# Attention stages on half-array tiles: two heads side by side in place of block-diagonal q and padded v

## Chip, cores, metric

One core of one Trainium2 chip. The metric is the device time of one execution in microseconds (us). A ratio is the mean time of one kernel's fast runs over the mean of the other's in the same rounds, so it is not quite the ratio of the medians that stand beside it.

## The reference

Block-wise linear attention with decay, over 4 batches, 8 heads, 768 positions and head size 64, and then a feed-forward layer with `h * cos(h)` between 512, 2048 and 512 columns. Cut to what matters:

```python
for b in range(nb):                       # blocks of 64 along the sequence
    intra = einsum('bhic,bhjc->bhij', qb, kb) * Dmask
    intra = einsum('bhij,bhjd->bhid', intra, vb)
    inter = einsum('bhid,bhde->bhie', qb * lam_pow, kv_state)
    out[:, :, sl] = intra + inter
    kv_state = lam_block * kv_state + einsum('bhsd,bhse->bhde', kb * rev_pow, vb)
x = out.transpose(0, 2, 1, 3).reshape(3072, 512)
h = x @ w_in                              # 512 -> 2048
return (h * cos(h)) @ w_out               # 2048 -> 512
```

## The kernel before

The kernel takes the sequence in 24 blocks of 128 positions (6 a batch). A planner in Python orders all instructions of all engines before they are emitted; attention of later blocks is mixed with the feed-forward matmuls of earlier ones. A head is 64 wide and the array is 128 by 128, so heads go in pairs p, and the array is filled with zeros where the two heads of a pair must not mix: q is copied into a block-diagonal tile `q_bd`, v is scaled into a padded tile `v_pad`, the state `kv_bd` is block-diagonal too. Cuts are marked `...`.

```python
def prep_v():                                             # GpSimd, two instructions
    for i in range(2):
        nc.gpsimd.tensor_mul(v_pad[n % NV][:, i::2, i * D:(i + 1) * D], src[:, i::2, :],
                             v_scale[:, c, i::2]...to_broadcast([P, NP, D]))
...
def transposes_out(sides):                                # VectorE, PSUM to SBUF
    nc.vector.tensor_copy(live["qkT", n][:, sides], live["t", n][:, sides])

def transposes_bd():                                      # VectorE, SBUF to SBUF, two instructions
    for i in range(2):
        h = slice(i * D, (i + 1) * D)
        nc.vector.tensor_copy(q_bd[n % NQ][h, :, i, :], t[h, 0, :, :])

def scores(half):                                         # 2 matmuls of 256 columns
    t = bank("ps_s", [P, 4, P], F32)                      # one bank, two buffers
    for i in range(2):
        p = 2 * half + i
        nc.tensor.matmul(t[:, 2 * i:2 * i + 2, :], lhsT=live["qkT", n][:, 1, p, :],
                         rhs=q_bd[n % NQ][:, p, :, :], start=True, stop=True)
...
def update():                                             # 4 matmuls of 128 columns
    for p in range(NP):
        nc.tensor.matmul(kv_ps[:, p, :], lhsT=live["k_b", n][:, 2 * p:2 * p + 2, :], rhs=both, ...)

def values(half):                                         # 2 x (1 inter + 2 intra) matmuls of 128
    for p in (2 * half, 2 * half + 1):
        if c:
            nc.tensor.matmul(t[:, p, :], lhsT=kv_bd[(n - 1) % NK][:, p, :],
                             rhs=live["qkT", n][:, 0, p, :], start=True, stop=False)
        for i in range(2):
            nc.tensor.matmul(t[:, p, :], lhsT=v_pad[n % NV][:, 2 * p + i, :],
                             rhs=live["s_m", n][:, 2 * p + i, :], ...)
```

## Time and profile before

| | before |
|---|---|
| time, median | 235.72 us of 3 runs at first, 235.46 us of 4 with the changed kernel's |
| span of the profiled run | 233.6 us, granted clock 0.999 |
| TensorE busy | 220.6 us, 94% |
| VectorE, ScalarE, GpSimd busy | 63%, 46%, 31% |

TensorE's records overlap, so its busy share hides small gaps. The useful measure is the slot: the difference of the starts of two matmuls that follow each other. Two rows of the costliest groups (line, engine, operation, output and input, shapes, count, then busy us and mean ns):

```profile
L250 POOL TENSOR_TENSOR v_pad<-v_f,v_scale 128x256 bf16<-128x256 f32 x48 | 29.1, 626 | 46.7 <-PE ps_o L341 30.1
L303 DVE TENSOR_TENSOR s_m<-ps_s,mask 128x512 bf16<-128x512 f32 x48 | 31.3, 684 | 4.2 <-PE ps_s L296 4.1
```

GpSimd (POOL) makes v in two instructions of 0.63 us a block. VectorE (DVE) masks the scores, and the idle time before that is put down to the score matmuls.

### The profile page before, as it was taken

The page shows a single profiled execution, that of the slowest core. Times are in us where ns is not written, and L with a number is a line of the kernel's source. Part 1 is how long each engine was busy: PE and PEld are TensorE (multiplying, and loading weights), DVE is VectorE, ACT ScalarE, POOL GpSimd, SP SyncE. Part 2 cuts the span into 40 slices and gives each one's busy share as a digit, 9 for nine tenths or more (in the row PEclk, how much of TensorE's full clock was granted, in tenths as well). Part 3 has the DMA queues.
Part 4 walks back from the last instruction along what each step waited for, and adds up shares of the span by engine and source line. Part 5 has one row for each costly group of instructions (what it writes and reads, how often), then busy time and mean ns, then how long its engine had stood idle before and what let it go on. Part 6 is the DMA issues. An engine that isn't in the chain of part 4 may idle for free.

```text
span 233.6 us, 4414 instructions
## 1 busy us (share of the span) xinstructions
PE 220.6 (94%) x1698; PEld 131.2 (56%) x1698; DVE 148.3 (63%) x279; ACT 106.6 (46%) x179; POOL 71.7 (31%) x108
## 2 busy tenths in 40 slices
PE   4887998899999999999999999999999999999993
PEld 4777543457776655555555555555555454556541
DVE  5577487087999998986685585685674563423210
ACT  5453676123445464554444445345345435544420
POOL 2569200486758665333314314412000000000000
PEclk9999999999999999999999999999999999999999
DMA  6997999999999999999562110110011011111112
GB/s 123 222 198 120 208 191 203 225 219 217 254 222 248 222 219 225 243 218 201 137 158 68 48 45 1 48 46 8 37 48 45 0 48 45 45 45 48 45 45 90
DMA packets 82868, 29.64 MB, mean 127 GB/s; under 512 B 75552, under 2 KB 79904, under 8 KB 82848
## 3 DMA queue, kind: packets, MB, share of 16 engines
q1 hardware_dynamic: 78480, 25.05, 48.6%
q0 software_dynamic: 4224, 4.19, 11.0%
q8 instruction: 13, 0.21, 0.4%
q10 hardware_dynamic: 144, 0.13, 0.2%
q14 instruction: 7, 0.06, 0.1%
HBM read 27.27 MB, written 6.29 MB: 144 GB/s over the span
## 4 chain that ended last, share of the span: by engine, by line
PE 71%; DVE 11%; DMA 10%; POOL 3%; ACT 2%; issue 1%; POOLq 0%
PE ps_f L410 30%; PE ps_h L372 26%; DMA w_out_sb<-in_moe_w_out_dram 8%; PE ps_s L296 4%; PE ps_t L266 4%; PE ps_o L341 4%; DVE q_bd L277 3%; DVE g L385 3%; DVE s_m L303 2%; DVE qkT L271 2%; PE ps_o L338 1%; PE ps_kv L316 1%; DMA lam_bc<-in_lam_dram 1%; POOL w_in_sb L214 1%; DVE kv_bd L325 1%; POOL w_out_sb L217 1%
## 5 line engine op out<-in xcount | busy, mean ns | idle before, releaser
L379 ACT ACTIVATE cos<-ps_h,halfpi 128x512 f32<-128x512 f32 (+1 forms) x107 | 66.3, 624 | 73.5 <-PE ps_h L372 73.4
L385 DVE TENSOR_TENSOR g<-ps_h,cos 128x512 bf16<-128x512 f32 (+1 forms) x107 | 64.5, 609 | 49.2 <-ACT cos L379 48.0
L410 PE MATMUL ps_f<-w_out_sb,g 128*128 128x512 bf16 x368 | 92.8, 379 | 1.4 <-ACT o_sb L423 0.7
L372 PE MATMUL ps_h<-xT,w_in_sb 128*128 128x512 bf16 (+1 forms) x428 | 93.7, 347 | 0.1
L372 PEld LDWEIGHTS <-w_in_sb 128*128 128x128 bf16 x448 | 43.0, 98 | 36.0 <-issue 0.4
L410 PEld LDWEIGHTS <-g 128*128 128x128 bf16 x384 | 35.9, 98 | 34.4 <-issue 2.2
L250 POOL TENSOR_TENSOR v_pad<-v_f,v_scale 128x256 bf16<-128x256 f32 x48 | 29.1, 626 | 46.7 <-PE ps_o L341 30.1
L303 DVE TENSOR_TENSOR s_m<-ps_s,mask 128x512 bf16<-128x512 f32 x48 | 31.3, 684 | 4.2 <-PE ps_s L296 4.1
L235 POOL TENSOR_TENSOR q_s<-q_f,q_scale 128x512 bf16<-128x512 f32 x23 | 24.0, 1043 | 22.5 <-PE ps_f L410 18.7
L271 DVE COPY qkT<-ps_t 128x1024 bf16<-128x1024 bf16 (+1 forms) x28 | 17.2, 614 | 17.3 <-PE ps_t L266 16.9
L423 ACT COPY o_sb<-ps_f 128x512 f32<-128x512 f32 x23 | 13.5, 586 | 21.7 <-PE ps_f L410 21.7
L277 DVE COPY q_bd<-qkT 64x512 bf16<-64x512 bf16 x48 | 19.6, 409 | 0.7
L341 PE MATMUL ps_o<-s_m,v_pad 128*128 128x128 bf16 x192 | 19.7, 221 | 0.4 <-DVE s_m L303 0.4
L350 ACT CAST xT<-ps_o 128x512 bf16<-128x512 f32 x24 | 14.0, 585 | 13.1 <-PE ps_o L341 13.0
L296 PE MATMUL ps_s<-q_bd,qkT 128*128 128x256 bf16 x96 | 15.6, 279 | 2.7 <-DVE qkT L271 1.8
L244 POOL CAST k_b<-k_f 128x512 bf16<-128x512 f32 x20 | 12.4, 620 | 17.6 <-issue 13.3
L341 PEld LDWEIGHTS <-v_pad 128*128 128x128 bf16 x192 | 14.9, 99 | 3.5 <-issue 0.5
L338 PE MATMUL ps_o<-qkT,kv_bd 128*128 128x128 bf16 x80 | 15.3, 219 | 0.0
L296 PEld LDWEIGHTS <-qkT 128*128 128x128 bf16 x96 | 8.8, 99 | 9.7 <-DVE q_bd L277 2.2
L325 DVE CAST kv_bd<-ps_kv 64x256 bf16<-64x256 f32 x32 | 13.4, 418 | 1.2 <-PE ps_kv L316 1.0
L468 PE MATMUL ps_h<-ident 128*128 128x64 bf16 x226 | 12.1, 211 | 1.6 <-POOL ident masks.py:199 1.6
L468 PEld LDWEIGHTS <-ident 128*128 128x128 bf16 x226 | 10.8, 111 | 1.8 <-POOL ident masks.py:199 1.6
(39 smaller groups left out, 93.1 us busy)
## 6 DMA issues: line engine op xcount, KB each, us to landing
q_f<-in_q_dram SPq DMA_DIRECT2D x24, 256.0 KB, 4.8
k_f<-in_k_dram SPq DMA_DIRECT2D x24, 256.0 KB, 4.8
v_f<-in_v_dram SPq DMA_DIRECT2D x24, 256.0 KB, 4.9
out_dram<-o_sb SPq DMA_DIRECT2D x23, 256.0 KB, 2.0
w_in_sb<-in_moe_w_in_dram POOLq DMA_DIRECT2D x4, 512.0 KB, 8.4
w_out_sb<-in_moe_w_out_dram POOLq DMA_DIRECT2D x4, 512.0 KB, 15.5
out_dram<-o_sb SPq DMA_DIRECT2D x1, 128.0 KB, 1.7
out_dram<-o_sb ACTq DMA_DIRECT2D x1, 128.0 KB, 1.7
```

The lines of the kernel that those rows point to most:

```text
L235: eng.tensor_mul(t, live.pop(("q_f", n)), q_scale[:, c, :].unsqueeze(2).to_broadcast([P, H, D]))
L250: nc.gpsimd.tensor_mul(v_pad[n % NV][:, i::2, i * D:(i + 1) * D], src[:, i::2, :], v_scale[:, c, i::2].unsqueeze(2).to_broadcast([P, NP, D]))
L271: nc.vector.tensor_copy(live["qkT", n][:, sides], live["t", n][:, sides])
L277: nc.vector.tensor_copy(q_bd[n % NQ][h, :, i, :], t[h, 0, :, :])
L296: nc.tensor.matmul(t[:, 2 * i:2 * i + 2, :], lhsT=live["qkT", n][:, 1, p, :], rhs=q_bd[n % NQ][:, p, :, :], start=True, stop=True)
L303: nc.vector.tensor_mul(live["s_m", n][:, 4 * half:4 * half + 4, :], live.pop(("s", n, half)), mask.unsqueeze(1).to_broadcast([P, 4, P]))
L341: nc.tensor.matmul(t[:, p, :], lhsT=v_pad[n % NV][:, 2 * p + i, :], rhs=live["s_m", n][:, 2 * p + i, :], start=(i == 0 and c == 0), stop=( ...
L372: ins = nc.tensor.matmul(t[:, :cols], lhsT=w_in_sb[:, kd, f * P:(f + 1) * P], rhs=live["xT", i][:, kd, :cols], start=(kd == 0), stop=(kd = ...
L379: nc.scalar.activation(c[:, :cols], live["h", i, f][:, :cols], AF.Sin, bias=halfpi)
L385: nc.vector.tensor_mul(live["g", i][:, f, :cols], live.pop(("h", i, f))[:, :cols], live.pop(("c", i, f))[:, :cols])
L410: nc.tensor.matmul(live["f", i, j], lhsT=live["g", i][:, f, j * P:(j + 1) * P], rhs=w_out_sb[:, f, :], start=(f == 0), stop=(f == KF - 1))
L468: nc.tensor.matmul(idle_ps[:, :cols], lhsT=ident, rhs=ident[:, :cols], start=True, stop=True)
```

## The change

The intent is to let two heads use the array at the same time. Scores contract over 64 rows, so head 0 takes the upper half of the array's rows and head 1 the lower half. State and values have 64 output columns, so the two heads take the two halves of the columns. Then q needs no block-diagonal copy and v no padding. The diff, cut to its core:

```diff
-    BUFS = {... "ps_s": 2, ...}
+    BUFS = {... "ps_s": 1, ...}          # one buffer, now of two banks
-    v_pad = [...]; q_bd = [...]
...
         def prep_v():
-            for i in range(2):
-                nc.gpsimd.tensor_mul(v_pad[n % NV][:, i::2, i * D:(i + 1) * D], src[:, i::2, :], ...)
+            nc.gpsimd.tensor_mul(live["v_s", n], live.pop(("v_f", n)), ...)
...
-        def transposes_bd():
-            for i in range(2):
-                nc.vector.tensor_copy(q_bd[n % NQ][h, :, i, :], t[h, 0, :, :])
...
+        def scores():
+            t = bank("ps_s", [P, 2, NP, P], F32)
+            for p in range(NP):
+                for i, h in enumerate(halves):
+                    nc.tensor.matmul(t[:, i, p, :], lhsT=live["qkT", n][h, 1, p, :], rhs=live["qkT", n][h, 0, p, :], ...)
...
             def update():
                 for p in range(NP):
+                    for i, h in enumerate(halves):
+                        nc.tensor.matmul(kv_ps[h, p, :], lhsT=live["k_b", n][:, 2 * p + i, :],
+                                         rhs=live["v_s", n][:, 2 * p + i, :], ...)
...
+        def values():                     # all inter matmuls first, full array; then the tiles
+            for p in range(NP if c else 0):
+                nc.tensor.matmul(t[:, p, :], lhsT=kv_bd[(n - 1) % NK][:, p, :], rhs=live["qkT", n][:, 0, p, :], ...)
+            for p in range(NP):
+                for i, h in enumerate(halves):
+                    nc.tensor.matmul(t[h, p, :], lhsT=live["v_s", n][:, 2 * p + i, :], rhs=live["s_m", n][:, i, p, :], ...)
```

The planner's durations change as well: a stage on tiles is booked with 0.15 us on top, and the pacing constant of a block goes from 1.78 to 1.35 us.

More of the change, by code (lines that the diff above doesn't have):

```diff
@@ L14 @@
 ALU = mybir.AluOpType
+ATT = 1.35
 TILES = [4, 2, 4, 4, 4, 4, 2]
@@ L114 @@
     first = [sum(TILES[:i]) for i in range(len(TILES) + 1)]
-    BUFS = {"ld": 4, "tok": 3, "ps_t": 1, "ps_s": 2, "ps_o": 1, "ps_h": 2, "ps_f": 1, "cos": 2, "o_sb": 3}
+    BUFS = {"ld": 4, "tok": 3, "ps_t": 1, "ps_s": 1, "ps_o": 1, "ps_h": 2, "ps_f": 1, "cos": 2, "o_sb": 3}
     ctx.enter_context(tc.manual_schedule())
@@ L140 @@
     nc.vector.memset(halfpi, math.pi / 2.0)
-    NV, NQ, NK = 3, 2, 2
-    v_pad = [consts.tile([P, H, P], BF16, name=f"v_pad{i}") for i in range(NV)]
-    q_bd = [consts.tile([P, NP, 2, P], BF16, name=f"q_bd{i}") for i in range(NQ)]
+    NK = 2
     kv_bd = [consts.tile([P, NP, P], BF16, name=f"kv_bd{i}") for i in range(NK)]
-    for t in v_pad + q_bd + kv_bd:
+    for t in kv_bd:
         nc.vector.memset(t, 0.0)
@@ L163 @@
     WCH = 4
-    kv_ps = psum.tile([P, NP, P], F32, tag="ps_kv", name="ps_kv")
-    pl = Planner({"ps_t": 1, "ps_s": 2, "ps_o": 1, "ps_h": 2, "ps_f": 1, "cos": 2, "o_sb": 3,
-                  "q_f": 4, "k_f": 4, "v_f": 4, "q_s": 3, "k_b": 3, "qkT": 3, "s_m": 3})
+    kv_ps = psum.tile([P, NP, D], F32, tag="ps_kv", name="ps_kv")
+    pl = Planner({**BUFS, "q_f": 4, "k_f": 4, "v_f": 4, "q_s": 3, "k_b": 3, "v_s": 3, "qkT": 3, "s_m": 3})
     MM = lambda cols, n=1: n * (cols / 2400.0 + 0.0025)
+    SW = 0.15
+    halves = [slice(i * D, (i + 1) * D) for i in range(2)]
     live = {}
-    unit = [MM(n * P, 4 * KF) + MM(DM, KF * n) + 1.78 * n for n in TILES]
+    unit = [MM(n * P, 4 * KF) + MM(DM, KF * n) + ATT * n for n in TILES]
     begins = [sum(unit[:i]) for i in range(len(unit) + 1)]
@@ L223, in add_w @@
         _, w_t[which, c] = dma("POOL", 2.6, 0.9, emit, prio, deps)
-    prep, T, To, Tb, Sc, So, V, Vo, U, Uo = ({} for _ in range(10))
+    prep, T, To, Sc, So, V, Vo, U, Uo = ({} for _ in range(9))
     def add_attention(n):
@@ L247, in prep_v @@
         def prep_v():
-            src = live.pop(("v_f", n))
-            for i in range(2):
-                nc.gpsimd.tensor_mul(v_pad[n % NV][:, i::2, i * D:(i + 1) * D], src[:, i::2, :],
-                                     v_scale[:, c, i::2].unsqueeze(2).to_broadcast([P, NP, D]))
+            live["v_s", n] = toks.tile([P, H, D], BF16, tag="v_s", name="v_s")
+            nc.gpsimd.tensor_mul(live["v_s", n], live.pop(("v_f", n)),
+                                 v_scale[:, c, :].unsqueeze(2).to_broadcast([P, H, D]))
         a = pl.add("DVE" if n == 0 else "POOL", 0.69 if n == 0 else 1.05, [load_t["q_f", n]], prep_q, pa(-0.9), get="q_s")
@@ L256, in add_attention @@
         issue_t["k_f", n].frees = [b]
-        d = pl.add("POOL", 1.2, [load_t["v_f", n], V.get(n - NV), U.get(n - NV)], prep_v, pa(-0.9))
+        d = pl.add("POOL", 1.05, [load_t["v_f", n]], prep_v, pa(-0.9), get="v_s")
         issue_t["v_f", n].frees = [d]
@@ L271, in transposes_out @@
             nc.vector.tensor_copy(live["qkT", n][:, sides], live["t", n][:, sides])
-        def transposes_bd():
-            t = live["qkT", n]
-            for i in range(2):
-                h = slice(i * D, (i + 1) * D)
-                nc.vector.tensor_copy(q_bd[n % NQ][h, :, i, :], t[h, 0, :, :])
         Tq = pl.add("PE", MM(P, 4), [a], lambda: transposes(0), pa(-0.05), get="ps_t")
@@ L288, in add_attention, with scores_out @@
         Tq.frees = [To[n]]
-        Tb[n] = pl.add("DVE", 0.6, [first_out, Sc.get((n - NQ, 1))], transposes_bd, pa(-0.01 if early else 0.1))
-        for half in range(2):
-            def scores(half=half):
-                t = bank("ps_s", [P, 4, P], F32)
-                for i in range(2):
-                    p = 2 * half + i
-                    nc.tensor.matmul(t[:, 2 * i:2 * i + 2, :], lhsT=live["qkT", n][:, 1, p, :],
-                                     rhs=q_bd[n % NQ][:, p, :, :], start=True, stop=True)
-                live["s", n, half] = t
-            def scores_out(half=half):
-                if half == 0:
-                    live["s_m", n] = toks.tile([P, H, P], BF16, tag="s_m", name="s_m")
-                nc.vector.tensor_mul(live["s_m", n][:, 4 * half:4 * half + 4, :], live.pop(("s", n, half)),
-                                     mask.unsqueeze(1).to_broadcast([P, 4, P]))
-            Sc[n, half] = pl.add("PE", MM(2 * P, 2), [Tb[n], To[n]], scores, pa(0.2 + 0.1 * half), get="ps_s")
-            So[n, half] = pl.add("DVE", 0.69, [Sc[n, half]] + ([So[n, 0]] if half else []), scores_out,
-                                 pa(0.25 + 0.1 * half), get=None if half else "s_m")
-            Sc[n, half].frees = [So[n, half]]
+        def scores():
+            t = bank("ps_s", [P, 2, NP, P], F32)
+            for p in range(NP):
+                for i, h in enumerate(halves):
+                    nc.tensor.matmul(t[:, i, p, :], lhsT=live["qkT", n][h, 1, p, :], rhs=live["qkT", n][h, 0, p, :],
+                                     start=True, stop=True)
+            live["s", n] = t
+        def scores_out(i):
+            if i == 0:
+                live["s_m", n] = toks.tile([P, 2, NP, P], BF16, tag="s_m", name="s_m")
+            nc.vector.tensor_mul(live["s_m", n][:, i], live["s", n][:, i], mask.unsqueeze(1).to_broadcast([P, NP, P]))
+        Sc[n] = pl.add("PE", MM(P, 4) + SW, [first_out, To[n]], scores, pa(0.2), get="ps_s")
+        for i in range(2):
+            So[n, i] = pl.add("DVE", 0.69, [Sc[n]] + ([So[n, 0]] if i else []), partial(scores_out, i),
+                              pa(0.25 + 0.1 * i), get=None if i else "s_m")
+        Sc[n].frees = [So[n, 0], So[n, 1]]
         if c < NB - 1:
@@ L313, in update @@
                 for p in range(NP):
-                    vp = v_pad[n % NV][:, 2 * p, :]
-                    both = bass.AP(tensor=vp.tensor, offset=vp.offset, ap=[list(vp.ap[0]), [P + D, 2], [1, D]])
-                    nc.tensor.matmul(kv_ps[:, p, :], lhsT=live["k_b", n][:, 2 * p:2 * p + 2, :], rhs=both,
-                                     start=(c == 0 and p == 0), stop=True, skip_group_check=True)
+                    for i, h in enumerate(halves):
+                        nc.tensor.matmul(kv_ps[h, p, :], lhsT=live["k_b", n][:, 2 * p + i, :],
+                                         rhs=live["v_s", n][:, 2 * p + i, :],
+                                         start=(c == 0 and p == 0), stop=True, skip_group_check=True)
@@ L319, in update_out @@
             def update_out():
-                for i in range(2):
-                    h = slice(i * D, (i + 1) * D)
-                    if early:
-                        nc.scalar.copy(kv_bd[n % NK][h, :, h], kv_ps[h, :, h])
-                    else:
-                        nc.vector.tensor_copy(kv_bd[n % NK][h, :, h], kv_ps[h, :, h])
+                for h in halves:
+                    (nc.scalar.copy if early else nc.vector.tensor_copy)(kv_bd[n % NK][h, :, h], kv_ps[h])
             last = next((Uo[m] for m in (n - 1, n - 2) if m in Uo), None)
-            U[n] = pl.add("PE", MM(P, 4), [b, d, last], update, pa(0.3))
+            U[n] = pl.add("PE", MM(D, 4) + SW, [b, d, last], update, pa(0.3))
@@ L329, in add_attention @@
             Uo[n] = pl.add("ACT" if early else "DVE", 0.85, [U[n], V.get(n - NK + 1)], update_out, pa(0.4))
         b.frees = [T[n]] + ([U[n]] if c < NB - 1 else [])
-        def values(half):
-            if half == 0:
-                live["o", n] = bank("ps_o", [P, NP, P], F32)
-            t = live["o", n]
-            for p in (2 * half, 2 * half + 1):
-                if c:
-                    nc.tensor.matmul(t[:, p, :], lhsT=kv_bd[(n - 1) % NK][:, p, :],
-                                     rhs=live["qkT", n][:, 0, p, :], start=True, stop=False)
-                for i in range(2):
-                    nc.tensor.matmul(t[:, p, :], lhsT=v_pad[n % NV][:, 2 * p + i, :],
-                                     rhs=live["s_m", n][:, 2 * p + i, :],
-                                     start=(i == 0 and c == 0), stop=(i == 1))
+        def values():
+            t = live["o", n] = bank("ps_o", [P, NP, P], F32)
+            for p in range(NP if c else 0):
+                nc.tensor.matmul(t[:, p, :], lhsT=kv_bd[(n - 1) % NK][:, p, :], rhs=live["qkT", n][:, 0, p, :],
+                                 start=(p == 0), stop=False, skip_group_check=True)
+            for p in range(NP):
+                for i, h in enumerate(halves):
+                    nc.tensor.matmul(t[h, p, :], lhsT=live["v_s", n][:, 2 * p + i, :], rhs=live["s_m", n][:, i, p, :],
+                                     start=(p == 0 and c == 0), stop=True, skip_group_check=True)
@@ L350, in values_out @@
             nc.scalar.copy(live["xT", i][:, :, j * P:(j + 1) * P], live.pop(("o", n)))
-        v0 = pl.add("PE", MM(P, 6 if c else 4), [So[n, 0], d, Uo.get(n - 1) if c else None],
-                    lambda: values(0), pa(0.5), get="ps_o")
-        V[n] = pl.add("PE", MM(P, 6 if c else 4), [So[n, 1], v0], lambda: values(1), pa(0.6))
+        V[n] = pl.add("PE", MM(P, 8 if c else 4) + SW, [So[n, 0], So[n, 1], d, Uo.get(n - 1) if c else None],
+                      values, pa(0.5), get="ps_o")
         So[n, 0].frees = [V[n]]
-        first_out.frees = [V[n]]
+        first_out.frees = [V[n], Sc[n]]
+        d.frees = [V[n]] + ([U[n]] if c < NB - 1 else [])
         Vo[n] = pl.add("ACT", 0.6, [V[n]] + ([h_last[i - 2]] if i >= 2 else []), values_out, pa(0.7))
-        v0.frees = [Vo[n]]
+        V[n].frees = [Vo[n]]
     h_last, o_last, hid_t = {}, {}, {}
@@ L407, in project @@
                     if f0 == 0:
-                        live["f", i, j] = bank(tag, [P, DM], F32)
+                        live["f", i, j] = bank("ps_s", [P, 2, DM], F32)[:, 0, :] if tag == "ps_s" else bank(tag, [P, DM], F32)
                     for f in range(f0, f0 + U4):
```

## The prediction

> **What bounds the kernel now.** I read the page first, then the chain, the engine shares by window, the timelines of TensorE and VectorE, and the waits. The page gives the suspect: the matmul engine is busy for 94% of the span, at full clock throughout.
>
> ```profile
> PE 220.6 (94%) x1698; PEld 131.2 (56%) x1698; DVE 148.3 (63%) x279; ACT 106.6 (46%) x179; POOL 71.7 (31%) x108
> ...
> PE   4887998899999999999999999999999999999993
> ...
> DVE  5577487087999998986685585685674563423210
> ```
>
> A busy PE need not be full, because matmul records overlap, so I count slots from starts in the timeline. These are PE rows (start, duration, operation) of one attention block among feed-forward matmuls, from late in the run:
>
> ```profile
> 131.36 0.22 PE L338 MATMUL ps_o<-qkT,kv_bd 128*128 128x128 bf16 x1
> 131.42 0.27 PE L341 MATMUL ps_o<-s_m,v_pad 128*128 128x128 bf16 x2
> ...
> 132.03 1.03 PE L372 MATMUL ps_h<-xT,w_in_sb 128*128 128x512 bf16 x4
> 132.90 0.39 PE L266 MATMUL ps_t<-ident,q_s 128*128 128x128 bf16 x4
> 133.12 1.03 PE L410 MATMUL ps_f<-w_out_sb,g 128*128 128x512 bf16 x4
> ...
> 136.79 0.39 PE L316 MATMUL ps_kv<-v_pad,k_b 128*128 128x128 bf16 x4
> 137.02 1.03 PE L410 MATMUL ps_f<-w_out_sb,g 128*128 128x512 bf16 x4
> 137.88 0.60 PE L296 MATMUL ps_s<-q_bd,qkT 128*128 128x256 bf16 x4
> 138.32 1.03 PE L372 MATMUL ps_h<-xT,w_in_sb 128*128 128x512 bf16 x4
> ```
>
> Differences of starts: four matmuls of 512 columns take 0.865 us (216 ns each), four of 256 take 0.44 us, four of 128 take 0.22 to 0.23 us (56 ns each), and the twelve of the values stage take 132.03 - 131.36 = 0.67 us. An attention block therefore occupies PE for 0.446 (eight transposes) + 0.437 (scores) + 0.223 (state) + 0.67 (values) = 1.78 us.
>
> Is PE really full? From 45 us to the last matmul's end, about 227 us in the chain, there are 182 us. In them fall the 384 projections less the 20 issued before, 364 x 0.216 = 78.7; the hidden layer without the first tile's 64, 256 x 0.216 + 128 x 0.109 = 69.3; and 20 blocks (numbers 4 to 23) x 1.78, less 7 absent state or inter stages of 0.223, = 34.0. The sum is 182: PE has next to no hole from 45 us on. I find holes of some 2.6 us in its timeline, all between 47 and 89 us, so the count is right to about 1%.
>
> The first 45 us are another matter: attention of the first four blocks, then the first hidden tile, and then the wait for the second weight matrix.
>
> ```profile
> 24.04 18.26 DMA w_out_sb<-in_moe_w_out_dram
> 42.34 1.04 PE ps_f L410 x4
> ```
>
> In that stretch the DMA engines are 99% busy; no attention arithmetic makes this arrive sooner. From about 201 us no attention is left. So the change can act on PE between 45 and 201 us, on 20 of 24 blocks. VectorE is nearly full as well between 60 and 85 us:
>
> ```profile
> 60.00:65.00 5.00, 5.00 (x54) 4.00 (x53) 4.88 (x12) 2.43 (x6) 3.41 (x5) 1.00 1.19 252
> 65.00:70.00 5.00, 4.63 (x50) 3.73 (x49) 4.88 (x11) 2.23 (x6) 2.82 (x4) 1.00 0.98 222
> 70.00:75.00 5.00, 4.80 (x49) 3.57 (x48) 4.88 (x12) 2.33 (x7) 4.26 (x7) 1.00 1.08 241
> ```
>
> (The columns are the window, its length, then busy us of PE, weight load, DVE, ACT and POOL.) That is where the holes lie.
>
> **What the Trainium skill says.** (1) "TensorE: Matmul & The Clock Gate", section "Back-to-back issue gap": a warm matmul of N columns takes N/2.4 + 2.5 ns. The trace agrees: 216 ns at 512 and 56 ns at 128. (2) The same page, section "Part 3: Packing small matmuls", says that matmuls on different tiles start about 4 ns apart and run together; nothing in this trace uses tiles. (3) "TensorEngine Tiling (Array Packing)", section "Key Properties": "Changing tiling mode (not just tile) drains the TensorE". No duration is given, and the trace has no switch. (4) The same page, section "Restrictions": column tiling disables fast weight load. Every load in this trace is the full 128x128 form, so what a 64-column load costs is not to be seen here either. Points 3 and 4 are the uncertainty of this case.
>
> One number can be read from the trace, though: how fast small load-and-matmul pairs go at all. The 64-column keep-awake matmuls, each with its own weight load:
>
> ```profile
> 21.21 0.66 PE L468 MATMUL ps_h<-ident 128*128 128x64 bf16 x17
> ...
> 23.47 0.31 PE L468 MATMUL ps_h<-ident 128*128 128x64 bf16 x5
> ```
>
> Twelve more take 0.35 us: 29 ns for one load plus matmul, and I take that as the pace that tiled instructions cannot beat.
>
> **The change, part by part.** Scores: four matmuls of 256 columns against a half-zero q become eight of 128 on two half-row tiles. Perfect pairs would take 4 x 56 = 0.223 us; at 29 ns an instruction 8 x 29 = 0.233. Saved: 0.437 - 0.233 = 0.204 us. State update: four matmuls of 128 columns become eight of 64 on two half-column tiles. Perfect pairs would take 0.117 us, but eight at 29 ns take 0.233: saved -0.01. Values: eight of 128 with padded v become eight on half-column tiles, 0.233 for 0.446: saved 0.213. The four inter matmuls and the transposes stay. Over the 20 blocks (16 with an update): 20 x 0.204 - 16 x 0.01 + 20 x 0.213 = 8.2 us off PE before any drain. A block then costs about 1.37 us; the diff's new pacing constant of 1.35 (1.78 before) fits that.
>
> Against it stand the switches. Neighbours in the PE order are full-array matmuls, so each tiled stage has one switch in and one out: (20 + 16 + 20) x 2 = 112. Each costs d: 0 to perhaps 100 ns. The record of a lone matmul reaches about 160 ns beyond its slot (0.22 us against 0.056), which bounds what emptying the array should take without a reload of weights. The diff's planner books 0.15 us for each stage, thus 75 ns for a switch; it may be a cautious guess. I choose d = 35 ns as an estimate, 3.9 us in all. Net on PE: 8.2 - 3.9 = 4.3 us.
>
> VectorE loses the two copies into the block-diagonal q:
>
> ```profile
> L277 DVE COPY q_bd<-qkT 64x512 bf16<-64x512 bf16 x48 | 19.6, 409 | 0.7
> ```
>
> This is 19.6 us, or 0.8 us a block, and 0.8 to 1.4 us for a pair between 60 and 89 us, exactly where VectorE is full. The five start-up memsets (2.4 us) go as well, but the first q there waits for ACT. VectorE off the path is worth only the PE holes it causes: a third to a half of the 2.6 us, say 0.9. Against that, scores of a block now need both banks free and the values wait for both masked halves; with feed-forward work to fill in, I take zero. POOL forms v in one instruction of about 1.04 us (the q row's 1043 ns) instead of two of 0.61; POOL is 31% busy and worth nothing, except a few tenths before the issue of the second weight matrix, whose transfer is DMA-bound: zero. Evacuations and state copies keep their sizes.
>
> Sum: 4.3 + 0.9 = 5.2 us, so 235.7 - 5.2 = 230.5 us, about 2.2% less.
>
> **Rivals.** (a) Tiles overlap well and a switch is nearly free (d under 15 ns): 8.2 + 0.9 less up to 1.7, so 226.6 to 228.3 us. With perfect pairs even 225. For it: the tuned-looking 1.35. (b) The drains eat the gain: at d = 75 ns they are 8.4 us, and only the VectorE relief is left: about 235 us. For it: the planner's own 0.15 us. (c) Column-tile weight loads lose their fast form and cannot pair: at 53 ns each (the skill's 64/1.2, in section "LDWEIGHTS"; an estimate) eight loads take 0.43 us. The update then costs 0.2 us more than before and the values gain nothing; with the drains at 35 to 75 ns the result is 239 to 244 us. Against it: a change tuned this far would hardly be kept. (d) DMA, VectorE or ACT takes over as the bound: loads run at about 3.5 us a block (768 KB at 220 GB/s) against some 5 us a block on PE; VectorE loses more per block than PE does; ACT is at 46%. I give this little weight.
>
> **Range and chances.** Rival (a) about 35%, the middle and (b) about 50%, (c) 15%. The limit for faster is 231.0 us, just beyond my centre, hence 0.48; slower needs over 240.4 us, most of (c): 0.12. The range of 226 to 238 us holds (a) to (b) with part of (c).
>
> **What would show it.** In the timeline from 130 us on: slot lengths by start differences of scores (0.23 us plus two drains), update (0.23) and values (0.46), against 0.44, 0.22 and 0.67 before. Gaps of tens of ns at the first tiled matmul and the first full one after it are d. If eight update matmuls take 0.4 us, the load is the cause (c). If the VectorE share in 60 to 85 us does not fall, the relief was misjudged. I am wrong in kind if new waits of PE on s_m or ps_s appear past 90 us, or if the second weight matrix lands more than 1 us away from 42 us.

## The result and the profile after

| | before | after |
|---|---|---|
| time, median | 235.46 us (235.04 to 237.22, 4 runs) | 232.54 us (232.29 to 233.24, 4 runs) |
| ratio, 95% interval | | 0.9867 (0.982 to 0.9914) |
| span of the profiled run | 233.6 us | 230.9 us |

The changed kernel is 1.3% faster, by the 2% mark the same. The page after, with the busy row and the slices of TensorE and VectorE:

```profile
PE 220.2 (95%) x1889; PEld 120.9 (52%) x1889; DVE 127.2 (55%) x226; ACT 106.4 (46%) x179; POOL 68.0 (29%) x84
...
PE   4899998799999999999999999999999999999993
...
DVE  1455575157779796685575475575573453433210
```

TensorE is as busy as before (220.2 against 220.6 us), though it has far fewer columns to stream. VectorE lost 21 us. Where TensorE's time went is seen in its timeline, from late in the run (the values of one block, then the other stages of the next):

```profile
128.42 0.39 PE L324 MATMUL ps_o<-qkT,kv_bd 128*128 128x128 bf16 x4
128.73 0.41 PE L328 MATMUL ps_o<-s_m,v_s 128*64 128x128 bf16 x8
129.08 1.04 PE L358 MATMUL ps_h<-xT,w_in_sb 128*128 128x512 bf16 x4
129.95 0.39 PE L265 MATMUL ps_t<-ident,q_s 128*128 128x128 bf16 x4
...
132.99 1.03 PE L358 MATMUL ps_h<-xT,w_in_sb 128*128 128x512 bf16 x4
133.95 0.40 PE L288 MATMUL ps_s<-qkT 64*128 64x128 bf16 x8
134.28 0.32 PE L307 MATMUL ps_kv<-v_s,k_b 128*64 128x64 bf16 x8
134.53 1.04 PE L396 MATMUL ps_f<-w_out_sb,g 128*128 128x512 bf16 x4
135.40 1.03 PE L358 MATMUL ps_h<-xT,w_in_sb 128*128 128x512 bf16 x4
```

The figures joined by a star give the part of the array that an operation uses: 128\*128, 64\*128 (half the rows) or 128\*64 (half the columns); call that its mode. Read the starts. The four inter matmuls begin at 128.42 and should give way after 0.22 us, but the first tiled one begins 0.31 us later. The eight tiled ones hold the engine for 129.08 - 128.73 = 0.35 us, where four pairs side by side are worth 0.22. The values stage as a whole takes 0.66 us, against 0.67 before. Scores: 0.10 us of waiting before them (132.99 + 0.865 = 133.855, and they begin at 133.95) and 0.33 us in them, 0.43 together, against 0.44 before.

The starts of the single instructions in the trace say what these extra times are. Within a stage the two heads of a pair begin 3 to 4 ns apart, and the next pair follows 56 ns later (32 ns in the update): two heads run wholly side by side. At each change of mode, in either direction, there is a hole of 89 to 99 ns after the previous matmul's slot (one of 0.18 us among 99), 95 ns in the median. Summed from the first transposes of the fifth block to the last matmul:

| us | before | after |
|---|---|---|
| begin of this stretch | 44.89 | 43.82 |
| slots of all matmuls, at N/2400 + 0.0025 us each for N columns, a pair as one with the 3 to 4 ns between its heads | 181.54 | 171.86 |
| 99 changes of mode | - | 9.48 |
| the first pair of a stage, slower by 11 to 24 ns, and the like | 0.07 | 0.98 |
| holes over 50 ns | 2.80 | 0.45 |
| length to the start of the last matmul | 184.41 | 182.77 |

So the tiles save 9.7 us of slots, and the mode changes take 9.5 us of it back. With the slower first pairs (0.9 us) TensorE's own part comes out 0.7 us worse. What makes the kernel faster is the last but one row, the holes (2.35 us), and the earlier begin (1.07 us). Their sum less 0.7 is 2.7 us, which is what the span fell by.

The earlier begin has a trail in the record of GpSimd's DMA issues. In the changed kernel GpSimd issued the first part of the first weight matrix at 16.44 us, before at 17.48; from 17.5 to 20 us the DMA engines moved 107 GB/s in place of 11, and the last part of the second matrix landed at 41.23 us in place of 42.29. All runs go the same way: where GpSimd makes v in one instruction (e1, e2, e4, e6 to e9), the issue is at 16.15 to 16.5 us and the landing at 41.1 to 41.9; where it makes v in two (e3, e5, e10 to e12), at 17.3 to 18.0 and at 41.8 to 42.5. Of these e8 and e10 differ only in v and in what the planner books for it (16.15 and 41.17 us against 17.57 and 41.90), so v moves the landing. How much of the earlier begin that gives is not shown: e8 and e1 landed early and still reached their fifth block late, at 47.78 and 45.13 us.

The windows where VectorE was nearly full before (window, length, then busy us of PE, weight load, DVE, ACT, POOL):

```profile
60.00:65.00 5.00, 5.00 (x62) 3.43 (x60) 4.28 (x11) 2.57 (x7) 2.79 (x4) 1.00 1.01 227
65.00:70.00 5.00, 5.00 (x65) 3.58 (x63) 3.84 (x9) 2.59 (x7) 3.68 (x5) 1.00 1.20 257
70.00:75.00 5.00, 5.00 (x62) 3.65 (x61) 4.76 (x12) 2.29 (x6) 3.38 (x4) 1.00 0.95 202
```

VectorE fell from 14.6 to 12.9 of 15 us, and TensorE rose from 14.4 to 15.0. The second weight matrix still ends a wait of TensorE at about the same place, 1.07 us earlier (the line is from the timeline; its chain before is in the prediction):

```profile
41.27 1.02 PE L396 MATMUL ps_f<-w_out_sb,g 128*128 128x512 bf16 x4 [0.54 <-DMA w_out_sb<-in_moe_w_out_dram]
```

### The profile page after: what moved, and what is told of

Read it like the earlier page. It is cut to its first block, busy times and chain, and to the rows that moved or that the text cites. A ratio compares the mean times of both kernels' runs of the same rounds, so it can differ in the third digit from the quotient of the medians.

```text
span 230.9 us, 4730 instructions
## 1 busy us (share of the span) xinstructions
PE 220.2 (95%) x1889; PEld 120.9 (52%) x1889; DVE 127.2 (55%) x226; ACT 106.4 (46%) x179; POOL 68.0 (29%) x84
## 4 chain that ended last, share of the span: by engine, by line
PE 90%; DMA 4%; ACT 3%; DVE 1%; issue 1%; POOL 0%; SPq 0%; POOLq 0%
PE ps_h L358 35%; PE ps_f L396 33%; PE ps_t L265 5%; PE ps_o L328 4%; PE ps_s L288 4%; PE ps_h L454 2%; PE ps_kv L307 2%; PE ps_o L324 2%; DMA k_f<-in_k_dram 2%; PE ps_f L358 2%; DMA lam_bc<-in_lam_dram 1%; DMA out_dram<-o_sb 1%; DVE qkT L270 1%; ACT L156 1%; ACT L152 1%
## 5 line engine op out<-in xcount | busy, mean ns | idle before, releaser
L358 PEld LDWEIGHTS <-w_in_sb 128*128 128x128 bf16 x448 | 42.3, 98 | 40.2 <-issue 0.2
L396 PEld LDWEIGHTS <-g 128*128 128x128 bf16 x384 | 34.9, 98 | 35.1 <-issue 2.7
L295 DVE TENSOR_TENSOR s_m<-ps_s,mask 128x512 bf16<-128x512 f32 x48 | 31.9, 685 | 13.6 <-PE ps_s L288 12.5
L249 POOL TENSOR_TENSOR v_s<-v_f,v_scale 128x512 bf16<-128x512 f32 x24 | 25.0, 1043 | 37.1 <-PE ps_o L328 18.5
L265 PE MATMUL ps_t<-ident,q_s 128*128 128x128 bf16 x96 | 9.8, 227 | 2.0 <-DVE q_s L235 2.0
L288 PE MATMUL ps_s<-qkT 64*128 64x128 bf16 x192 | 9.7, 222 | 0.6 <-DVE qkT L270 0.3
L265 PE MATMUL ps_t<-ident,k_b 128*128 128x128 bf16 x96 | 9.6, 223 | 0.7 <-ACT k_b L242 0.3
L265 PEld LDWEIGHTS <-q_s 128*128 128x128 bf16 x96 | 7.0, 101 | 6.0 <-DVE q_s L235 2.2
L328 PE MATMUL ps_o<-s_m,v_s 128*64 128x128 bf16 x192 | 10.1, 228 | 0.0
L288 PEld LDWEIGHTS <-qkT 64*128 64x128 bf16 x192 | 5.5, 95 | 8.5 <-DVE g L371 3.8
## 6 DMA issues: line engine op xcount, KB each, us to landing
w_out_sb<-in_moe_w_out_dram POOLq DMA_DIRECT2D x4, 512.0 KB, 14.6
```

The source lines that it names most:

```text
L249: nc.gpsimd.tensor_mul(live["v_s", n], live.pop(("v_f", n)), v_scale[:, c, :].unsqueeze(2).to_broadcast([P, H, D]))
L265: nc.tensor.transpose(live["t", n][:, i, p, :], src[:, 2 * p:2 * p + 2, :], ident)
L288: nc.tensor.matmul(t[:, i, p, :], lhsT=live["qkT", n][h, 1, p, :], rhs=live["qkT", n][h, 0, p, :], start=True, stop=True)
L295: nc.vector.tensor_mul(live["s_m", n][:, i], live["s", n][:, i], mask.unsqueeze(1).to_broadcast([P, NP, P]))
L328: nc.tensor.matmul(t[h, p, :], lhsT=live["v_s", n][:, 2 * p + i, :], rhs=live["s_m", n][:, i, p, :], start=(p == 0 and c == 0), stop=True, ...
L358: ins = nc.tensor.matmul(t[:, :cols], lhsT=w_in_sb[:, kd, f * P:(f + 1) * P], rhs=live["xT", i][:, kd, :cols], start=(kd == 0), stop=(kd = ...
```

## The experiments

**Theory A**: a change of mode costs TensorE some 95 ns and eats what the pairs save; the gain is that VectorE's copies of q are gone. **Theory B**: the gain comes from the tiled array work, and VectorE's relief does little. All twelve are beside runs of the kernel before on the same chip:

| run | median us | before, same chip | ratio (95%) |
|---|---|---|---|
| e3 scores alone on tiles | 232.93 | 235.33 | 0.991 (0.987 to 0.996) |
| e4 values and state alone on tiles, one score buffer | 241.03 | 235.33 | 1.023 (1.018 to 1.027) |
| e5 before, q copies by ScalarE | 235.42 | 235.33 | 1.000 (0.997 to 1.003) |
| e7 stages joined | 230.36 | 235.33 | 0.979 (0.975 to 0.983) |
| e1 values interleaved | 245.5 | 235.64 | 1.042 (1.039 to 1.046) |
| e2 one head after the other | 233.85 | 235.64 | 0.993 (0.989 to 0.997) |
| e6 unread q copies back | 238.06 | 235.64 | 1.011 (1.009 to 1.014) |
| e8 before, values and state on tiles | 239.01 | 235.64 | 1.017 (1.011 to 1.024) |
| e9 unread q copies back, from PSUM | 234.88 | 235.31 | 0.998 (0.996 to 1.001) |
| e10 as e8, v in two instructions | 237.18 | 235.31 | 1.008 (1.006 to 1.010) |
| e11 before, q copies from PSUM | 234.43 | 235.31 | 0.996 (0.994 to 0.998) |
| e12 before, q copies left out (wrong) | 232.42 | 235.73 | 0.987 (0.984 to 0.991) |

### What a change of mode costs

**e1, the values stage in the old order.** The changed kernel, with the inter matmul of each pair next to the pair's tiles.

```diff
-            for p in range(NP if c else 0):
-                nc.tensor.matmul(... inter of p ...)
             for p in range(NP):
+                if c:
+                    nc.tensor.matmul(... inter of p ...)
                 for i, h in enumerate(halves):
```

> The changed kernel, same instructions; in the values stage the four full-array inter matmuls alternate with the four half-column pairs (as the kernel before ordered them) in place of all four first. Six mode changes more in each of the 17 blocks after 44 us that have an inter part. Theory A (96 ns for every change of mode): 102 x 0.096 = 9.8 us more than the changed kernel, 241.5 to 243 us. Rival (the hole belongs to the start of a stage, for instance a wait for its data or its first weights, not to the mode): no more than 1 us more.

Measured 245.5 us (2 runs), 13 us more than the changed kernel, with the same instructions. TensorE's timeline of one values stage:

```profile
136.71 0.22 PE L325 MATMUL ps_o<-qkT,kv_bd 128*128 128x128 bf16 x1
136.85 0.25 PE L328 MATMUL ps_o<-s_m,v_s 128*64 128x128 bf16 x2
137.03 0.23 PE L325 MATMUL ps_o<-qkT,kv_bd 128*128 128x128 bf16 x1
137.19 0.25 PE L328 MATMUL ps_o<-s_m,v_s 128*64 128x128 bf16 x2
137.37 0.23 PE L325 MATMUL ps_o<-qkT,kv_bd 128*128 128x128 bf16 x1
```

Every step takes 0.14 to 0.18 us where its slot is 0.056. After the fifth block's transposes there are 201 changes of mode in place of 99; the stretch to the last matmul is 11.1 us longer, and it begins 1.3 us later. A hole is 104 ns in the median here, 120 ns on the way back to the full array. The cost is one of the mode change, not of a stage's start. It was somewhat larger than I had expected (241.5 to 243 us).

**e7, the stages joined.** From block 12 on, values of block n-1, update and scores of block n are one unit in TensorE's order: inter, half-column tiles (values, update), half-row tiles (scores), then feed-forward again.

```diff
+            def joined(vals=vals, upd=upd, scores=scores):
+                vals()          # values of block n-1: inter, then 128*64
+                if upd:
+                    upd()       # update of block n: 128*64
+                scores()        # scores of block n: 64*128
+            Sc[n].emit = joined
```

> The changed kernel with values of block n-1, update and scores of block n issued back to back from block 12 on (inter matmuls, half-column tiles, half-row tiles), so three mode changes a block in place of five or so. Same instructions. Theory A: about 23 mode changes fewer at 96 ns, 2.2 us less than the changed kernel: 230.0 to 230.8 us. Theory B or a cost per stage rather than per mode change: no difference, 232.5 us.

Measured 230.36 us (229.59 to 231.39, 4 runs), as theory A says; the median is 2.2 us under the changed kernel's, which was timed in other rounds; the ratios to the kernel before are 0.979 and 0.987. The timeline of a joined unit:

```profile
129.76 0.39 PE L341 MATMUL ps_o<-qkT,kv_bd 128*128 128x128 bf16 x4
130.08 0.41 PE L345 MATMUL ps_o<-s_m,v_s 128*64 128x128 bf16 x8
130.33 0.29 PE L319 MATMUL ps_kv<-v_s,k_b 128*64 128x64 bf16 x8
130.55 0.40 PE L293 MATMUL ps_s<-qkT 64*128 64x128 bf16 x8
```

Values to update, both on half columns, takes 130.33 - 130.08 = 0.25 us: no mode change between them, no hole. In all 73 changes in place of 99. This is the fastest correct kernel. Joining all blocks was not run: the planner's own times put new holes before block 12, where the scores would have to wait for their transposes.

**e2, one head after the other.** In all three stages the four matmuls of head 0 come first, then the four of head 1 (in the built program: four on the first tile, four on the second).

```diff
-            for p in range(NP):
-                for i, h in enumerate(halves):
+            for i, h in enumerate(halves):
+                for p in range(NP):
```

> The changed kernel, same instructions and mode changes; in all three tiled stages the four matmuls of the first head's tile go first, then the four of the second head's, so neighbours in the order use the same half of the array. If only neighbours overlap: scores and values take about 0.40 us in place of 0.22, the update 0.22 in place of 0.12: 20 x 0.18 x 2 + 16 x 0.1 = 8.8 us more than the changed kernel, 240 to 242 us. If TensorE pairs matmuls on different halves wherever they stand in its queue: 232.5 us.

Measured 233.85 us (2 runs), not 240 to 242: the expectation failed. The timeline shows stages that are some 10 ns longer than in the changed kernel, not twice as long:

```profile
133.41 1.03 PE L358 MATMUL ps_h<-xT,w_in_sb 128*128 128x512 bf16 x4
134.37 0.41 PE L288 MATMUL ps_s<-qkT 64*128 64x128 bf16 x8
134.71 0.33 PE L307 MATMUL ps_kv<-v_s,k_b 128*64 128x64 bf16 x8
134.97 1.04 PE L396 MATMUL ps_f<-w_out_sb,g 128*128 128x512 bf16 x4
```

By single starts, matmuls again come in pairs, now 13 ns apart. The trace does not say on which tile a matmul is, but the length decides: one after the other on the first tile, then on the second, the eighth of a scores stage could begin no sooner than six slots (0.33 us) after the first, and it began 0.19 us after. The two heads need not be neighbours in the order; four on one tile do not hold up the four behind them on the other.

### Which part of the change brings the gain

**e3, scores alone on tiles.** The changed kernel with padded v, and full-array update and values.

```diff
-                        nc.tensor.matmul(t[h, p, :], lhsT=live["v_s", n][:, 2 * p + i, :], ...
+                        nc.tensor.matmul(t[:, p, :], lhsT=v_pad[n % NV][:, 2 * p + i, :], ...   # update likewise
```

> The changed kernel with the state update and the values put back on the full array (padded v); only the scores stay on half-row tiles, and the copies of q on VectorE stay away. Theory A (a change of tile mode holds TensorE 96 ns and eats what the pairs save; the gain is VectorE's, whose copies of q no longer hold up the scores): 40 mode changes in place of 99 after 44 us, score slots 0.21 us a block shorter, so 20 x 0.21 - 40 x 0.096 = 0.4 us saved on TensorE, holes of about 2.4 us gone and the front 1 us shorter: 232 to 233 us, as the changed kernel within 0.7 us. Theory B (the gain comes from the tiled array work, all three stages): only a third to a half of the gain of 2.9 us stays: 234 to 234.5 us.

Measured 232.93 us: the gain, within 0.4 us of the changed kernel, with 40 changes of mode. This is where q_bd goes away.

**e4 and e8, values and state alone on tiles.** e4 is the changed kernel with q_bd and full-array scores back; e8 is the kernel before with only values and state changed.

```diff
e4:  nc.tensor.matmul(t[:, p // 2, 2 * (p % 2):2 * (p % 2) + 2, :], lhsT=..., rhs=q_bd[n % NQ][:, p, :, :])   # and transposes_bd back
e8:  scores as before; prep_v, update, values as in the changed kernel
```

> The changed kernel with the scores put back on the full array, with block-diagonal q and its two VectorE copies; values and state stay on half-column tiles. Theory A: slots fall by 6.2 us over 20 blocks (0.11 in each of 16 updates, 0.22 in each of 20 values), some 72 mode changes take 6.9 us plus about 0.8 us of slow first pairs, and the holes from VectorE and the longer front stay: no gain, 235.5 to 237 us. Theory B: half to two thirds of the gain: 233.5 to 234 us.

> The kernel before with values and state on half-column tiles and nothing else changed: block-diagonal q, its copies and the two half-size score buffers stay. (The earlier run of this part also had the one two-bank score buffer of the changed kernel, and came out at 241 us.) Theory A: slots 6.2 us less, some 70 mode changes 6.7 us more, slow first pairs 0.5 us more, holes and front as before: 235.5 to 237 us. If column tiles were themselves the loss seen in that earlier run: 239 us or more.

Measured 241.03 and 239.01 us, both slower than the kernel before and slower than theory A's numbers; e8 came out at the number of its rival, that column tiles are themselves the loss. Something was missing in the theory; e8's profile shows one thing at 16 to 21 us (timeline, all engines, other lines left out):

```profile
16.15 0.94 POOL L215 DMA_DIRECT2D w_in_sb<-in_moe_w_in_dram  x1
...
16.48 3.65 DVE L277 COPY q_bd<-qkT 64x512 bf16<-64x512 bf16 x2
...
17.10 1.06 POOL L236 TENSOR_TENSOR q_s<-q_f,q_scale 128x512 bf16<-128x512 f32 x1
18.09 0.80 POOL L215 DMA_DIRECT2D w_in_sb<-in_moe_w_in_dram  x1
18.91 1.05 POOL L250 TENSOR_TENSOR v_s<-v_f,v_scale 128x512 bf16<-128x512 f32 x1
...
20.64 0.61 PE L296 MATMUL ps_s<-q_bd,qkT 128*128 128x256 bf16 x2 [3.09 <-DVE qkT L271]
```

Two copies that take 0.58 us when alone took 3.65 us here, and TensorE stood for 3.09 us; its mean granted clock was 0.89 over the first 30 us. The profiled run is the slowest of e8's four, 242.15 us at a mean clock of 0.986; the others took 238.59 to 239.07 us at 0.998 to 1.000. So the low clock does not explain the median of 239.01.

### What the copies of q do to VectorE

The same happens in the kernel before, on a smaller scale. Its copies, by the view of that tile (count, then min, median and max ns), and one of them in the timeline:

```profile
L277 DVE COPY q_bd<-qkT x48: 273/291/1143, 7.4 to 186.9; 64x512 bf16<-64x512 bf16 x48
```

```profile
47.04 1.04 POOL L235 TENSOR_TENSOR q_s<-q_f,q_scale 128x512 bf16<-128x512 f32 x1
47.13 1.40 DVE L277 COPY q_bd<-qkT 64x512 bf16<-64x512 bf16 x2
...
48.59 0.38 PE L296 MATMUL ps_s<-q_bd,qkT 128*128 128x256 bf16 x2 [0.49 <-DVE q_bd L277]
```

GpSimd is at work until 48.08; the first copy, begun at 47.13, ends at 48.22, the second takes its usual 0.29, and the scores wait. Of the 48 copies 16 took over 295 ns. All but one ended 141 to 153 ns after the end of a GpSimd instruction that was running when they began (the other, of 312 ns, 90 ns after). The Trainium skill has this in "SBUF — State Buffer", section "Who interferes with whom": VectorE and GpSimd share one port pair, a VectorE copy in a two-port mode takes it, and the one that comes second waits for the whole instruction of the first. The trace agrees where GpSimd computes, though no view names the copy's mode; two copies that began during a DMA issue of GpSimd took their usual 0.29 us. Theory A now has two parts: the copies cost VectorE time and a step ahead of the scores, and they are locked out by GpSimd.

**e5, the copies on ScalarE** (full array, blocks from the fifth on).

```diff
-                nc.vector.tensor_copy(q_bd[n % NQ][h, :, i, :], t[h, 0, :, :])
+                (nc.vector.tensor_copy if early else nc.scalar.copy)(q_bd[n % NQ][h, :, i, :], t[h, 0, :, :])
```

> The kernel before, all on the full array, with one edit: from the fifth block on, the two copies into block-diagonal q are made by ScalarE in place of VectorE (first four blocks as before, so the front is unchanged). Theory A: the TensorE holes of 2.4 to 2.9 us between 47 and 89 us mostly close: 233 to 234 us, with no tile in the program. Theory B: 235.5 us, unchanged. If ScalarE, which has the cosines as well, becomes late there, holes move and the time stays; then it tells nothing.

Measured 235.42 us, no gain; the expectation of theory A failed. A ScalarE copy takes 615 ns, so the step ahead of the scores became 1.23 us, behind the cosines in ScalarE's order. In 60 to 90 us TensorE was busy for 28.1 us, against 29.0 before. Freeing VectorE by making another engine late proves nothing either way.

**e6 and e9, unread copies put back** into the changed kernel, from SBUF and from PSUM.

```diff
+        def copies_unused():
+            for i, h in enumerate(halves):
e6:              nc.vector.tensor_copy(q_x[n % 2][h, :, i, :], live["qkT", n][h, 0, :, :])
e9:              nc.vector.tensor_copy(q_x[n % 2][h, :, i, :], live["t", n][h, 0, :, :])
```

> The changed kernel with the two copies of q per block put back on VectorE, into a tile that nobody reads: the load on VectorE is back, but the scores do not wait for the copies other than by VectorE's order. If VectorE's load made the holes in TensorE: about 235 us, and the holes of some 2.4 us between 47 and 89 us are back. If the copy as a step between transposes and scores made them: 232.5 to 233.2 us.

> As the run that put the two unread copies of q back on VectorE, except that they read q from PSUM (the transposes) and not from SBUF. In the trace of the kernel before, a copy from SBUF to SBUF that starts while GpSimd works lasts until some 145 ns after GpSimd's instruction (up to 1143 ns, against 273 to 291), while copies from PSUM are always 424 or 690 ns. If VectorE's hours were the cause, the result is that of the run with SBUF copies, 236.5 to 239 us, for a PSUM copy is no shorter (about 0.42 us each). If the lock-out by GpSimd was the cause: 232.5 to 234 us.

Measured 238.06 and 234.88 us, so 5.5 and 2.3 us above the changed kernel. The copies from PSUM are longer when alone, yet never held up:

```profile
L300 DVE COPY q_x<-ps_t x48: 405/422/428, 7.2 to 186.2; 64x512 bf16<-64x512 bf16 x48
```

Those from SBUF took up to 1960 ns. Neither expectation fits alone: e6 lies above both of its numbers, e9 between its two. The copies count with no lock-out at all, about 2 us, and from SBUF they cost about 3 us more. In e6 the front came late, the mean clock of the first 30 us was 0.94, and that of the whole run 0.990 to 0.993 in all five runs (0.996 to 1.000 in e9), so what of the 3 us is the lock-out itself and what the lower clock is not taken apart. One reservation: in e9 the copies also keep the transposes' PSUM buffer, and TensorE waited 1.5 us for that, so e9 is not VectorE's time alone.

**e10, v in two GpSimd instructions** (e8 otherwise).

```diff
-            nc.gpsimd.tensor_mul(live["v_s", n], live.pop(("v_f", n)), ...)
+            for i in range(2):
+                nc.gpsimd.tensor_mul(live["v_s", n][:, i::2, :], src[:, i::2, :], ...)
```

> The kernel before with values and state on half-column tiles (239 us), with GpSimd forming v in two instructions of about 0.6 us as the kernel before does, in place of one of 1.04 us. If longer GpSimd instructions, which lock VectorE's q copies out for longer, made that kernel slower than before: 235.5 to 237 us. If the loss was in the tiled work: 239 us still.

Measured 237.18 us, 1.8 us less than e8, just above the upper number of the first alternative. Shorter GpSimd instructions, shorter lock-outs. The rest of the loss is the tiles', by the same sum as above on e10's trace, from the fifth block on against before: slots 5.7 us less, 68 changes of mode 6.8 us more, first pairs 0.9 us more, holes 0.2 us less, and a begin 0.4 us earlier. That makes 1.4 us, as do the spans of the profiled runs (235.0 against 233.6 us); the medians differ by 1.9.

**e11, block-diagonal q straight from PSUM** (full array, no tiles).

```diff
-            t = live["qkT", n]
+            t = live["t", n]
```

> The kernel before, full array, no tiles; VectorE makes block-diagonal q straight from the transposes in PSUM in place of from their SBUF copy: the same count of copies, each longer when alone (about 0.42 against 0.28 us), never locked out by GpSimd. If the lock-out made TensorE's holes and the longer front: 233 to 234 us, the greater part of the change's gain without a tile. If VectorE's load made them: 235.5 to 237 us.

Measured 234.43 us, 0.9 us less than before, between the two expectations. From the fifth block on, TensorE's holes over 50 ns fell from 2.80 to 1.30 us without any tile; but that stretch began 1.0 us later, for the transposes' buffer was now held by the copies (TensorE's waits for that: 2.8 us in all).

**e12, the copies left out.** The kernel before, full array; q_bd stays zero, so the result is wrong, and all other instructions stay.

```diff
-        Tb[n] = pl.add("DVE", 0.6, [first_out, Sc.get((n - NQ, 1))], transposes_bd, ...)
+        Tb[n] = first_out
```

> The kernel before, full array, no tiles, with the copies into block-diagonal q left out: it stays all zero, so the result is wrong on purpose; every matmul and every other instruction stays. This takes the copies away whole (their step between transposes and scores, their time on VectorE, and their lock-outs with GpSimd), where two earlier runs only moved them. If the copies' absence is what the change gains and the tiles come out even: 232 to 233 us, as the changed kernel. If the tiles bring part of the gain themselves: 234 us or more.

Measured 232.42 us, ratio 0.987 (0.984 to 0.991); the changed kernel has 0.987 (0.982 to 0.991). Slots are the 181.54 us of the kernel before to the last digit, and the holes over 50 ns fall from 2.80 to 0.08 us. TensorE in the windows of interest:

```profile
60.00:65.00 5.00, 5.00 (x58) 4.26 (x56) 4.25 (x10) 2.69 (x6) 3.39 (x5) 1.00 1.08 242
65.00:70.00 5.00, 5.00 (x54) 3.87 (x52) 4.86 (x12) 2.21 (x5) 2.85 (x6) 1.00 1.00 233
70.00:75.00 5.00, 5.00 (x60) 4.27 (x58) 4.83 (x11) 2.25 (x5) 4.27 (x7) 1.00 1.26 221
```

TensorE is full. VectorE is still busy for 13.9 of these 15 us (14.6 before), but from 60 to 90 us it fell from 29.1 to 24.9 us, much as in the changed kernel (24.1). So the run shows what the copies cost as a whole; it does not tell VectorE's time from the step in front of the scores or from the lock-out. The zeros in q_bd did not change the granted clock: 0.996 to 1.000, as in the kernel before. With the slots of full-array work the gain is there, which settles A against B. The equal ratios hide unequal sums, though: without the copies the holes gave 2.7 us and the begin 0.2; in the changed kernel the holes gave 2.35, the begin 1.07, and the tiles with their mode changes cost 0.7.

## Why the prediction was right or wrong

The time, 232.5 us, is within the range of 226 to 238 us and 2 us above the centre of 230.5. My first guess, faster by over 2% at 0.48, was not met; within 2%, at 0.40, is what came. The bound was named rightly, and so were the stretch in which the change can act and the candidates, but the terms of the sum were mis-sized and their errors partly cancelled, so that the time fell inside the range partly by luck. (Of the sums, 364 x 0.216 is 78.6, not 78.7, which changes nothing.)

- **"The pace that tiled instructions cannot beat"**, 29 ns, held for 128 columns (28 ns an instruction) but not for the update, where a pair takes 32 ns, 16 an instruction. The saving of slots was 9.7 us, not 8.2. The update gained where I had -0.01.
- **"I choose d = 35 ns"** is the step that failed most. It measured 95 ns. The count was nearly right (99 against 112; eleven times two tiled stages of different mode follow each other, which saves one change each, and once two of the same mode, which saves two). Drains took 9.5 us, not 3.9. I had bounded it by the 160 ns tail of a lone matmul and then chosen a value well under half of that, with the planner's 75 ns in view. Rival (b), that the drains eat the gain, is what happened on TensorE: -9.7 of slots, +9.5 of mode changes, +0.9 of slower first pairs, +0.7 us together where I had -4.3.
- **VectorE's relief, "say 0.9"**, was taken at a third to a half of the holes. It was 2.35 of 2.8 us, and 2.7 in e12. I had seen pairs of copies of 0.8 to 1.4 us where 0.58 is usual and not asked what stretched them; that was the sign of GpSimd's lock-out.
- **The front, "no attention arithmetic makes this arrive sooner" and "zero"**: the stretch from the fifth block began 1.07 us earlier. The first hidden tile began 1.5 us earlier (23.37 against 24.90 us), and the weights' wait ended 1.07 us earlier. I had taken the front as bound by the DMA, but from 17.5 to 20 us the engines' busy share was 0.12 (11 GB/s); in the changed kernel, with GpSimd's issue 1.04 us earlier, it was 0.69. The earlier tile is not enough: e12 had it too (23.04), with the issue at 17.50 us, and won only 0.22 us at the fifth block. GpSimd's v, which I had called worth nothing, moves the landing (e8 against e10), and is the likely cause. The second matrix landed at 41.23 us, within the 1 us around 42 that I had named.
- **Rival (c)**, slow weight loads on half columns, did not occur: the eight loads and matmuls of an update took 0.25 us with the hole after them, 0.15 without it. (Its 53 ns a load are from "TensorE: Matmul & The Clock Gate", section "LDWEIGHTS". Its sum was off as well: with the 0.9 us of relief that the other sums contain, it comes to 238 to 242 us, not 239 to 244.) Rival (d) neither. Rival (a) had the pairs right and the switch wrong.
- I looked for new waits of TensorE on s_m or on the single score buffer after 90 us; there are none.

Still open: how the 95 ns divide between emptying the array and loading weights that could not be loaded ahead (no run tells these apart), and how the copies' cost of about 3 us divides between VectorE's time, lock-out and their mere place ahead of the scores (e6, e9, e10, e11 and e12 show them mixed, none purely).

## What to carry to other kernels

Count changes of tile mode before tiling small matmuls: at about 95 ns each, a switch in and a switch out (0.19 us) eat nearly all that four pairs of 128 columns save (0.22 us), so put tiled stages of the same mode next to each other, as e7 does. Look at the spread of one instruction form's durations, not only its mean; a copy that takes 273 ns at best and 1143 at worst is waiting for someone. And when a change removes work from two engines, run it with each removal alone before crediting the one it was made for.

## What the Trainium skill lacked or had wrong

- "TensorEngine Tiling (Array Packing)", "Key Properties", gives no time for the drain at a change of mode. Here: 89 to 99 ns in the changed kernel (99 changes, median 95), 104 ns in the median where the mode changes after every one or two matmuls (e1), in either direction and between half rows and half columns alike.
- "TensorE: Matmul & The Clock Gate", "Part 3: Packing small matmuls", says that matmuls start in strict program order. With four on one tile ahead of four on the other (e2) they still began in pairs, 13 ns apart and 56 ns from pair to pair. Its 4 ns for neighbours agrees: 3 to 4 ns.
- The same page, "Back-to-back issue gap", also gives sustained figures of about 81 ns for 128 and 131 ns for 512 columns with weight loads. Here streams with one load for each matmul ran at 56 and 216 ns, the page's other formula.
- That half-column tiles lose fast weight load had no visible cost beyond a stage's first pairs (80 ns where 56 is usual in the values, 53 where 32 is usual in the update; the half-row scores, which the restriction does not name, have 67); later pairs of the update came every 32 ns with two loads each. The tiling page names the restriction without its size.
- "SBUF — State Buffer", "Who interferes with whom", is borne out. It lacks the tail for a copy that waits on GpSimd: it ended 141 to 153 ns after GpSimd's instruction. And in e8 a copy lasted through two GpSimd instructions in a row, a DMA issue and a multiplication (1.84 us).
